# Expert preparation inside the attention's tail: where tiles lie, who prepares the first inputs, and which engine computes z from chunk 8

## The chip, the cores and the metric

The kernel runs on one core of a Trainium2 chip. A core has a matrix engine (TensorE, PE in the profile, with PEld for its weight loads), three engines for elementwise work (VectorE or DVE, ScalarE or ACT, GpSimd or POOL) and SyncE (SP), which here only issues DMAs. Each engine takes its instructions strictly in the order in which they stand in its own queue; semaphores make it wait for others. The metric is the device time of one execution in microseconds (us), lower is better.

## The reference

Two stages follow each other: a linear recurrence over 768 tokens for 4 batches of 8 heads (state 40x40), and then a mixture of 8 experts on the 3072 tokens of 320 features that come out of it, weighted by a matrix P that is normalised eight times over rows and columns.

```python
def _attn_ref(r, k, v, w, a, b):            # 4, 8, 768, 40 each
    for t in range(S):
        y[:, :, t] = np.einsum('bhd,bhde->bhe', rt, state)
        Sa = np.einsum('bhde,bhe->bhd', state, at)
        state_decay = state * wt[:, :, None, :] - np.einsum('bhd,bhe->bhde', Sa, bt)
        state = state_decay + np.einsum('bhd,bhe->bhde', vt, kt)

def _moe_ref(x, w_gate, w1, w2):            # x 3072x320, 8 experts, 1024 hidden
    logits = x @ w_gate
    P = np.exp(logits - logits.max())
    for _ in range(8):
        P /= P.sum(1, keepdims=True) + 1e-09
        P /= P.sum(0, keepdims=True) + 1e-09
        P *= N / E
    for e in range(E):
        out += P[:, e:e + 1] * (np.maximum(x @ w1[e], 0.0) @ w2[e])
```

## The kernel before

**Attention.** The 768 tokens are cut into 12 chunks c of 64; the 4 batches b run interleaved, so that there are 48 recurrence steps. `prep` builds a chunk's matrices, groups of two chunks invert their triangular systems on VectorE (`inv_diag`, `contract`, `finish`, L182 to L365), the result goes to DRAM and back, and `tmat` (L250) makes the matrix tt from it. A recurrence step (`recur`, L268) is a chain over the engines: matmul av (L282), mask f on VectorE (L283), matmuls xc (L290), copies to x and c on ScalarE (L296, L297), matmul pu (L301), mask pm on VectorE (L303), matmul c (L308), sum ws on VectorE (L310). From ws two things follow: y (L314, GpSimd), the output, which goes to the DRAM tensor xd (L317) and into the gate matmuls lp (L338); and z (L323), the state for the next chunk, which is transposed (L328) and copied into rv on ScalarE (L330, L331). Only z is on the recurrence. It is computed by GpSimd up to chunk 8 and by VectorE from chunk 9; chunk 11 has none. The steps load rv and f from DRAM through SyncE (L271, L273).

**Experts.** Weights come in 60 pieces k (`prep_w`, L498): one load of 832 KB into a raw tile ws, four sums on GpSimd (ss, 128x256 each), casts into wh by ScalarE, and remainders by GpSimd (L519 to L529; wl and a strip of wh). Tokens come in quarters s, each of three parts u (`prep_x`, L531): loads from xd into xs, four differences xt (L545 to L550), casts into xch by ScalarE (L547, L552, L555) and remainders xcl and a strip of xch (L553 to L561). For quarter 0 all of `prep_x` but the casts is on VectorE. A block is one k for one quarter: `layer1` has 28 matmuls (L573) in seven products, sums on VectorE (L591, L597) and ReLU on ScalarE (L594); `layer2` has 36 matmuls (L638). There are 128 blocks, 8192 matmuls. `sinkhorn` (L650) normalises P while the first blocks run; it needs the last gate logits lg.

**What sets the order.** Up to block 8 (N_MAN) a list scheduler with a timeline of its own orders the instructions of every engine, attention and experts together; from block 8 on, the order is the one in which the code is written. An expert tile is placed by its pool on memory that an attention tile has held, and may be written only when the readers of that tile are done. In the kernel before, the pools stand in the order stg, x0, hp, x1 (L472 to L496), and the two raw weight tiles take turns.

Of the kernel before, what the change touches and what calls it, by code (L numbers as in the profile page):

```python
# [11 lines left out]
F32 = mybir.dt.float32  # L12
F32R = mybir.dt.float32r
# [16 lines left out]
def attention(ctx, tc, d, xd, ps, pq, pt, gs, lg):  # L30
    nc = tc.nc
    pin = ctx.enter_context(tc.tile_pool(name="a_in", bufs=1))
    inv = ctx.enter_context(tc.tile_pool(name="a_inv", bufs=1))
    sets = [ctx.enter_context(tc.tile_pool(name=f"a_set{i}", bufs=1)) for i in range(NSX)]
# [233 lines left out]
    def recur(c, b):  # L268
# [54 lines left out]
        (nc.vector if c >= 9 else nc.gpsimd).tensor_tensor(out=z, in0=ws[:, :, 64:104],  # L323
# [28 lines left out]
    gq, gcount = deque(), [0]  # L352
# [103 lines left out]
def body(ctx, tc, d, out):  # L456
# [9 lines left out]
    with ExitStack() as actx:  # L466
# [3 lines left out]
        attention(actx, tc, d, xd, ps, pq, pt, gs, lg)  # L470
# [5 lines left out]
    two = ctx.enter_context(tc.tile_pool(name="two", bufs=1))  # L476
# [10 lines left out]
    xch, xcl, whs, wls = [], [], [], []
    for i in range(NWS):
        if i < SC:
            pool = x1 if i else x0  # L490
            xch.append(pool.tile([128, 7, 2, 384], F32R, name=f"xch{i}"))
            xcl.append(pool.tile([128, 7, 384], F32R, name=f"xcl{i}"))
        pool = x0 if i < 2 else x1
        whs.append(pool.tile([128, 2432], F32R, name=f"wh{i}"))
        wls.append(pool.tile([128, 1536], F32R, name=f"wl{i}"))
    acc = x1.tile([128, NT * SC, DM], F32, name="acc")  # L496

    def prep_w(k):  # L498
        e, f = (k // FP if k < E * FP else 2 * E - 2 - k // FP), k % FP
        raw = stg.tile([128, 1664], F32, name="ws")  # L500
        nc.sync.dma_start(out=raw, in_=d["wts"][e, f])
        yield
        so = stg.tile([128, 4, 2, 128], F32, name="ss", bufs=1)
# [323 lines left out]
```

## Time and profile before

| | us |
|---|---|
| median of 3 runs | 1811.9 (1807.26 to 1816.87) |
| the profiled execution | 1813.25 |
| its span in the trace | 1811.3 |
| busy in the span: PE / PEld | 1691.7 / 1668.9 |
| busy in the span: DVE / POOL / ACT | 1361.3 / 868.8 / 842.0 |
| mean granted clock of PE | 0.951 |

Times in the trace count from the start of the span. A row of the timeline has the start, the duration, the engine, the line, the operation, output and inputs, the shape and how many instructions were merged; in brackets stands how long the engine idled before it and what it waited for. A matmul group x8 of this trace is four matmuls in the code. A row of the stage table has the stage, its length, then for PE, PEld, DVE, ACT and POOL the busy time and the number of instructions, the granted clock of PE (1.00 is full speed), the share of DMA engines busy, and GB/s.

### The profile page before, as it was taken

The page shows a single profiled execution, that of the slowest core. Times are in us where ns is not written, and L with a number is a line of the kernel's source. Part 1 is how long each engine was busy: PE and PEld are TensorE (multiplying, and loading weights), DVE is VectorE, ACT ScalarE, POOL GpSimd, SP SyncE. Part 2 cuts the span into 40 slices and gives each one's busy share as a digit, 9 for nine tenths or more (in the row PEclk, how much of TensorE's full clock was granted, in tenths as well). Part 3 has the DMA queues.
Part 4 walks back from the last instruction along what each step waited for, and adds up shares of the span by engine and source line. Part 5 has one row for each costly group of instructions (what it writes and reads, how often), then busy time and mean ns, then how long its engine had stood idle before and what let it go on. Part 6 is the DMA issues. An engine that isn't in the chain of part 4 may idle for free.

```text
span 1811.3 us, 32736 instructions
## 1 busy us (share of the span) xinstructions
PE 1691.7 (93%) x12611; PEld 1668.9 (92%) x12611; DVE 1361.3 (75%) x2353; ACT 842.0 (46%) x1811; POOL 868.8 (48%) x850
## 2 busy tenths in 40 slices
PE   5468978898889999999999999999999999999999
PEld 4368878898888999999999999999999999999999
DVE  6887986974788677768686778867686777767675
ACT  6357767756534443434343444345343443434342
POOL 7555645614553453719173553009173553719160
PEclk8569989987899999999999999999999999999999
DMA  8478688577311111102010112202010111102001
GB/s 200 106 152 199 161 178 200 141 149 180 107 44 39 39 39 38 58 20 76 19 58 25 53 39 72 58 1 76 20 57 25 52 39 39 58 20 76 19 20 44
DMA packets 178737, 135.61 MB, mean 75 GB/s; under 512 B 119190, under 2 KB 160790, under 8 KB 178582
## 3 DMA queue, kind: packets, MB, share of 16 engines
q1 hardware_dynamic: 174901, 127.79, 27.1%
q10 hardware_dynamic: 3680, 5.74, 1.2%
q8 instruction: 99, 1.62, 0.4%
q14 instruction: 57, 0.46, 0.1%
HBM read 111.48 MB, written 22.02 MB: 74 GB/s over the span
## 4 chain that ended last, share of the span: by engine, by line
PE 75%; DVE 11%; DMA 5%; issue 3%; POOL 2%; SPq 2%; ACT 2%; ACTq 0%; DVEq 0%; POOLq 0%
PE op L638 36%; PE p L573 34%; DVE pr L194 1%; PE xc L290 1%; DVE q L128 1%; DMA lu<-ld 1%; PE pu L301 1%; SPq L248 1%; DMA inp<-in_inp_dram 1%; DVE un L197 1%; DMA rv<-in_rv_dram 1%; DVE sm L591 1%; DVE gt L197 1%; POOL ab L154 1%; DMA ld<-lt 1%
## 5 line engine op out<-in xcount | busy, mean ns | idle before, releaser
L573 PE MATMUL p<-xch,wh 128*128 128x384 f32 (+1 forms) x1792 | 605.9, 339 | 8.4 <-DVE sm L591 4.3
L594 ACT ACTIVATE hh<-sm 128x384 fp32r<-128x384 f32 x512 | 269.4, 527 | 729.9 <-DVE sm L591 729.9
L638 PE MATMUL op<-wh,hh 128*128 128x320 f32 x1536 | 477.2, 311 | 3.5 <-ACT hh L594 3.3
L638 PE MATMUL op<-wl,hh 128*128 128x320 f32 x1536 | 475.0, 310 | 0.0
L638 PE MATMUL op<-wh,hl 128*128 128x320 f32 x1536 | 468.9, 310 | 0.9 <-DVE hl L597 0.9
L519 POOL TENSOR_TENSOR wl<-ws,wh 128x640 fp32r<-128x640 f32 x60 | 102.8, 1714 | 608.9 <-ACT wh L517 608.7
L597 DVE SCALAR_TENSOR_TENSOR hl<-sm,hh 128x384 fp32r<-128x384 f32 x512 | 368.5, 753 | 1.9 <-ACT hh L594 1.3
L573 PEld LDWEIGHTS p<-xch,wh 128*128 128x128 f32 (+1 forms) x1792 | 337.7, 189 | 12.6 <-DVE sm L591 5.2
L573 PE MATMUL p<-xcl,wh 128*128 128x384 f32 x896 | 302.9, 338 | 0.0
L573 PE MATMUL p<-xch,wl 128*128 128x384 f32 x896 | 302.1, 337 | 0.0
L638 PEld LDWEIGHTS op<-wh,hh 128*128 128x128 f32 x1536 | 290.3, 189 | 4.4 <-ACT hh L594 4.4
L638 PEld LDWEIGHTS op<-wl,hh 128*128 128x128 f32 x1536 | 291.1, 190 | 0.0
L638 PEld LDWEIGHTS op<-wh,hl 128*128 128x128 f32 x1536 | 287.8, 188 | 1.3 <-DVE hl L597 1.2
L591 DVE TENSOR_TENSOR sm<-p,u 128x384 f32<-128x384 f32 x384 | 237.8, 629 | 8.9
L573 PEld LDWEIGHTS p<-xcl,wh 128*128 128x128 f32 x896 | 169.0, 189 | 0.0
L573 PEld LDWEIGHTS p<-xch,wl 128*128 128x128 f32 x896 | 168.9, 189 | 0.0
L591 DVE TENSOR_TENSOR sm<-p,p 128x384 f32<-128x384 f32 x128 | 71.3, 557 | 129.7 <-PE p L573 77.9
L591 DVE TENSOR_TENSOR p<-p,p 128x384 f32<-128x384 f32 x128 | 71.1, 555 | 103.5 <-PE p L573 103.1
L591 DVE TENSOR_TENSOR u<-p,p 128x384 f32<-128x384 f32 x128 | 70.8, 553 | 61.0 <-PE p L573 59.7
L527 POOL TENSOR_TENSOR wl<-ss,wh 128x512 fp32r<-128x512 f32 x60 | 90.2, 1503 | 31.5 <-ACT wh L524 27.4
L160 PE MATMUL ll<-ab,kb 104*128 104x128 f32 x336 | 62.0, 342 | 43.3 <-POOL ab L155 24.3
L160 PEld LDWEIGHTS ll<-ab,kb 104*128 104x128 f32 x336 | 53.9, 244 | 48.7 <-POOL ab L155 27.4
(164 smaller groups left out, 2642.7 us busy)
## 6 DMA issues: line engine op xcount, KB each, us to landing
ws<-in_wts_dram SPq DMA_DIRECT2D x60, 832.0 KB, 4.5
inp<-in_inp_dram SPq DMA_DIRECT2D x42, 451.5 KB, 4.7
rv<-in_rv_dram SPq DMA_DIRECT2D x48, 336.0 KB, 5.0
xd<-y SPq DMA_DIRECT2D x24, 224.0 KB, 2.9
ld<-lt ACTq DMA_DIRECT2D x40, 128.0 KB, 3.8
f<-in_vt_dram SPq DMA_DIRECT2D x48, 80.0 KB, 2.7
out_dram<-acc SPq DMA_DIRECT2D x42, 80.0 KB, 2.1
lu<-ld SPq DMA_DIRECT2D x24, 128.0 KB, 3.2
```

The costliest lines, as they stand in the source:

```text
L128: nc.vector.tensor_tensor_scan(out=qr.rearrange("r p t -> r (p t)"), data0=w65[:, 260:0:-1], data1=one65, initial=0.0, op0=ALU.mult, op1=A ...
L154: eng.tensor_tensor(out=ab[0:40, :, 0:64], in0=a_in[0:40], in1=g[0:40], op=ALU.mult)
L160: nc.tensor.matmul(ll[:, p], lhsT=kb[:, p], rhs=ab[:, p], start=True, stop=True)
L194: nc.vector.tensor_tensor(out=prv, in0=a.unsqueeze(2).broadcast_to([nu, n_c, n_r, n_k]), in1=m.unsqueeze(1).broadcast_to([nu, n_c, n_r, n_ ...
L197: nc.vector.tensor_reduce(out=dst, in_=prv, op=ALU.add, axis=AX.X)
L519: g.tensor_tensor(out=wl[:, 0:640], in0=raw[:, 256:896], in1=wh[:, 0:640], op=ALU.subtract)
L527: g.tensor_tensor(out=lv[:, 3:7], in0=so[:, :, 0], in1=hv[:, 3:7, 0], op=ALU.subtract)
L573: nc.tensor.matmul(o, lhsT=w_, rhs=x_, start=(j == 0), stop=(j == 3))
L591: eng.tensor_tensor(out=out, in0=x, in1=y, op=ALU.add)
L594: nc.scalar.activation(out=hh[:, f, h], in_=sm[f][:, h], func=AF.Relu)
L597: v.scalar_tensor_tensor(out=hl[:, f, h], in0=sm[f][:, h], scalar=0.0, in1=hh[:, f, h], op0=ALU.max, op1=ALU.subtract)
L638: nc.tensor.matmul(ops[i], lhsT=a[:, h, cs], rhs=w_[:, cw], start=(f == 0 and h == 0 and j == 0), stop=(last and h == 1 and j == 2))
```

## The change

Three edits, and what the scheduler makes of them.

1. Memory. Each expert tile gets a pool of its own (helper `pool`, with waits on the single attention tiles under it), and the pools stand in another order: xs, xt, the first token pair, the first raw weight tile, ss, the first weight pair, the work tiles of layer 1, and so on. The pool `a_inv` of attention moves to between set 6 and set 7. Pieces 0, 1 and 2 of the weights all use raw tile 0; from piece 3 on, the two take turns.
2. Who prepares. For quarter 0 GpSimd does all of `prep_x`, the casts too (nine new casts on GpSimd). The first two weight pieces and quarter 0 stand under `tc.issue_after(ends)`, where `ends` is GpSimd's last z: what they put on GpSimd's queue stands behind that instruction.
3. z is on VectorE from chunk 8 on, not from chunk 9. So GpSimd's last z is that of chunk 7, batch 3.

```diff
+    sets = []
+    for i in range(NSX):
+        if i == 7:
+            inv = ctx.enter_context(tc.tile_pool(name="a_inv", bufs=1))
+        sets.append(ctx.enter_context(tc.tile_pool(name=f"a_set{i}", bufs=1)))
...
-        (nc.vector if c >= 9 else nc.gpsimd).tensor_tensor(out=z, in0=ws[:, :, 64:104],
+        ends["z" if c < 8 else "v"] = (nc.vector if c >= 8 else nc.gpsimd).tensor_tensor(out=z, in0=ws[:, :, 64:104],
...
+    return ends["z"].ins
...
-    stg = ctx.enter_context(tc.tile_pool(name="stg", bufs=2))
-    x0 = ctx.enter_context(tc.tile_pool(name="x0", bufs=1))
-    hp = ctx.enter_context(tc.tile_pool(name="hp", bufs=2))
-    x1 = ctx.enter_context(tc.tile_pool(name="x1", bufs=1))
+    def pool(name, **kw):
+        return ctx.enter_context(tc.tile_pool(name=name, bufs=1, reuse_waits="tile", **kw))
...
+    xs_t = [pool(f"xs{i}").tile([128, 2, 2, 256], F32, name=f"xs{i}") for i in range(2)]
+    xt_t = pool("xt").tile([128, 4, 2, 128], F32, name="xt")
+    x_pair(0)
+    raws = [pool("ws0").tile([128, 1664], F32, name="ws0")]
+    ss_t = pool("ss").tile([128, 4, 2, 128], F32, name="ss")
+    w_pair(0)
...
-        raw = stg.tile([128, 1664], F32, name="ws")
+        raw = raws[k % 2 if k > 2 else 0]
...
-        v = nc.vector
+        v = nc.vector if s else nc.gpsimd
+        copy = nc.scalar.copy if s else nc.gpsimd.tensor_copy
...
-        nc.scalar.copy(out=xh[:, 0:3, :, cu], in_=bv)
+        copy(out=xh[:, 0:3, :, cu], in_=bv)
...
-    run(prep_w(0), prep_w(1), *(prep_x(0, u) for u in range(3)))
+    with tc.issue_after(ends):
+        run(prep_w(0), prep_w(1), *(prep_x(0, u) for u in range(3)))
```

Up to chunk 8 the queues of both kernels hold the same instructions in the same order. From there they differ at three places. Numbers behind an underscore are the scheduler's tile numbers; the changed file's lines are shifted (z is L326, y L317, product L597, weight load L524).

**GpSimd at chunk 8** (st_ and ge_ are the chunk's decay tiles, y_214 and y_215 the output tiles). Before:

```order
L314 TENSOR_TENSOR y_214<-ws,st_149 104x4x64
L323 TENSOR_TENSOR z<-ws,cc_155 104x160
L314 TENSOR_TENSOR y_214<-ws,st_150 104x4x64
L323 TENSOR_TENSOR z<-ws,cc_159 104x160
L314 TENSOR_TENSOR y_215<-ws,st_151 104x4x64
L323 TENSOR_TENSOR z<-ws,cc_163 104x160
L314 TENSOR_TENSOR y_215<-ws,st_152 104x4x64
L323 TENSOR_TENSOR z<-ws,cc_167 104x160
L314 TENSOR_TENSOR y_214<-ws,ge_156 104x4x64
L314 TENSOR_TENSOR y_214<-ws,ge_160 104x4x64
L314 TENSOR_TENSOR y_215<-ws,ge_164 104x4x64
L314 TENSOR_TENSOR y_215<-ws,ge_168 104x4x64
```

Now, from the same y on:

```order
L317 TENSOR_TENSOR y_214<-ws,st_149 104x4x64
L569 TENSOR_TENSOR xt<-xs_5504 128x256
L570 TENSOR_TENSOR xt<-xs_5504 128x256
L573 TENSOR_TENSOR xt<-xs_5504,xt 128x256
L574 TENSOR_TENSOR xt<-xs_5504,xt 128x256
L317 TENSOR_TENSOR y_214<-ws,st_150 104x4x64
L571 CAST xch_5516<-xs_5504 128x6x128
L576 CAST xch_5516<-xt 128x4x128
L579 CAST xch_5516<-xt 128x4x128
L571 CAST xch_5516<-xs_5508 128x6x128
L577 TENSOR_TENSOR xcl_5517<-xs_5504,xch_5516 128x3x128
L580 TENSOR_TENSOR xch_5516<-xs_5504,xch_5516 32x3x128
```

The four z are gone from the queue and the token preparation stands between the outputs y. Between this first y and the last y of attention there are now 61 instructions of the experts; before there were 26 of them, the first one behind ge_168.

**PE at chunk 10** (sx_169 is a step's matrix; p_5683 and p_5695 are the first two products of block 0). Before:

```order
L290 MATMUL xc_4977<-f,sx_169 104x104 x4
L290 MATMUL xc_4978<-f,sx_169 104x104 x4
L282 MATMUL av<-rv_208 104x128 x4
L328 MATMUL zt<-cst,z 40x104 x4
L257 MATMUL gp<-lt_200 32x32 x32
L308 MATMUL c_5010<-pm,bb_166 104x104 x4
L263 MATMUL op<-t_201,mt 32x32 x32
```

Now:

```order
L293 MATMUL xc_4977<-f,sx_169 104x104 x4
L293 MATMUL xc_4978<-f,sx_169 104x104 x4
L597 MATMUL p_5683<-xch_5516,wh_5529 128x384
L597 MATMUL p_5695<-xch_5516,wh_5529 128x384
L285 MATMUL av<-rv_208 104x128 x4
L260 MATMUL gp<-lt_200 32x32 x32
L331 MATMUL zt<-cst,z 40x104 x4
L311 MATMUL c_5010<-pm,bb_166 104x104 x4
L597 MATMUL p_5683<-xcl_5517,wh_5529 128x384
L597 MATMUL p_5695<-xcl_5517,wh_5529 128x384
L266 MATMUL op<-t_201,mt 32x32 x32
```

The first expert matmul stands ahead of 328 attention matmuls, where it stood ahead of 88. In front of the last gate matmul there are 60 expert matmuls, before 55.

**SyncE where the first weights are loaded.** Before:

```order
L317 DMA xd<-y_215 448x1x128
L501 DMA ws<-in_wts_dram 128x1664 x2
L536 DMA xs<-xd 128x2x256
L538 DMA xs<-xd 32x2x256
L273 DMA f<-in_vt_dram 64x8x40
```

Now:

```order
L560 DMA xs_5504<-xd 128x2x256
L274 DMA rv_210<-in_rv_dram 112x4x192
L562 DMA xs_5504<-xd 32x2x256
L524 DMA ws_5521<-in_wts_dram 128x1664
L276 DMA f<-in_vt_dram 64x8x40
L274 DMA rv_211<-in_rv_dram 112x4x192
```

The first weight piece moves ahead, to between the loads rv_210 and rv_211 of an earlier step; the second stays near the old place, alone, behind the load rv_209; the third stands where the last steps' outputs are written.

More of the change, by code (lines that the diff above doesn't have):

```diff
@@ L350, in gate_step @@
                 gq.popleft()
-    gq, gcount = deque(), [0]
+    gq, gcount, ends = deque(), [0], {}
     ys = {}
@@ L469, in body, with w_pair, x_pair @@
         nc.sync.dma_start(out=gs, in_=d["gate"])
-        attention(actx, tc, d, xd, ps, pq, pt, gs, lg)
-    stg = ctx.enter_context(tc.tile_pool(name="stg", bufs=2))
-    x0 = ctx.enter_context(tc.tile_pool(name="x0", bufs=1))
-    hp = ctx.enter_context(tc.tile_pool(name="hp", bufs=2))
-    x1 = ctx.enter_context(tc.tile_pool(name="x1", bufs=1))
-    two = ctx.enter_context(tc.tile_pool(name="two", bufs=1))
+        ends = attention(actx, tc, d, xd, ps, pq, pt, gs, lg)
+    def pool(name, **kw):
+        return ctx.enter_context(tc.tile_pool(name=name, bufs=1, reuse_waits="tile", **kw))
+    def w_pair(i):
+        p = pool(f"w{i}")
+        whs[i] = p.tile([128, 2432], F32R, name=f"wh{i}")
+        wls[i] = p.tile([128, 1536], F32R, name=f"wl{i}")
+    def x_pair(i):
+        p = pool(f"x{i}")
+        xch[i] = p.tile([128, 7, 2, 384], F32R, name=f"xch{i}")
+        xcl[i] = p.tile([128, 7, 384], F32R, name=f"xcl{i}")
+    xch, xcl, whs, wls = [None] * SC, [None] * SC, [None] * NWS, [None] * NWS
+    xs_t = [pool(f"xs{i}").tile([128, 2, 2, 256], F32, name=f"xs{i}") for i in range(2)]
[4 more added lines that the diff above has]
+    w_pair(0)
+    hp = pool("hp")
+    sm_t = [hp.tile([128, 768], F32, name=f"sm{i}") for i in range(2)]
+    p_t = [hp.tile([128, 384], F32, name=x) for x in ("p1", "p5", "u2", "u3")]
+    hx = [pool("h0")]
+    w_pair(1)
+    w_pair(2)
+    raws.append(pool("ws1").tile([128, 1664], F32, name="ws1"))
+    wls[3] = pool("wl3").tile([128, 1536], F32R, name="wl3")
+    hx.append(pool("h1"))
+    hs = [tuple(p.tile([128, 2, 768], F32R, name=f"{x}{i}") for x in ("hh", "hl")) for i, p in enumerate(hx)]
+    x_pair(1)
+    whs[3] = pool("wh3").tile([128, 2432], F32R, name="wh3")
+    acc = pool("acc").tile([128, NT * SC, DM], F32, name="acc")
+    two = pool("two")
     pmat = two.tile([128, 24, E], F32, name="pmat")
@@ L481, in body @@
     nc.sync.dma_start(out=ident, in_=d["cst"][:, 232:360])
-    po = ctx.enter_context(tc.tile_pool(name="po", bufs=1, space=bass.MemoryType.PSUM))
+    po = pool("po", space=bass.MemoryType.PSUM)
     ops = [po.tile([128, DM], F32, name=f"op{i}") for i in range(4)]
-    pl = [ctx.enter_context(tc.tile_pool(name=f"pl{i}", bufs=1, space=bass.MemoryType.PSUM)) for i in range(2)]
-    pe = ctx.enter_context(tc.tile_pool(name="pe", bufs=1, space=bass.MemoryType.PSUM))
+    pl = [pool(f"pl{i}", space=bass.MemoryType.PSUM) for i in range(2)]
+    pe = pool("pe", space=bass.MemoryType.PSUM)
     ops += [pe.tile([128, DM], F32, name=f"op{i}") for i in range(4, NT)]
[L487 to L496, printed above, removed]
     def prep_w(k):
         e, f = (k // FP if k < E * FP else 2 * E - 2 - k // FP), k % FP
-        raw = stg.tile([128, 1664], F32, name="ws")
+        raw = raws[k % 2 if k > 2 else 0]
         nc.sync.dma_start(out=raw, in_=d["wts"][e, f])
         yield
-        so = stg.tile([128, 4, 2, 128], F32, name="ss", bufs=1)
+        so = ss_t
         a21, a11, a12, a22 = (raw[:, o:o + 256].rearrange("r (k m) -> r k m", k=2)
@@ L577, in layer1 @@
         v = nc.vector
-        hh = hp.tile([128, 2, 768], F32R, name="hh")
-        hl = hp.tile([128, 2, 768], F32R, name="hl")
-        sm = [hp.tile([128, 768], F32, name=f"sm{i}", bufs=1) for i in range(2)]
-        p1, p5, u2, u3 = (hp.tile([128, 384], F32, name=x, bufs=1) for x in ("p1", "p5", "u2", "u3"))
+        hh, hl = hs[n % 2]
+        sm, (p1, p5, u2, u3) = sm_t, p_t
         def prod(i):
```

10 lines of the change are left out of this document (4 added, 6 removed).

## The prediction

> **What bounds the kernel now.** I read the stages first. Columns: stage, length, busy time and number of instructions of PE, PEld, DVE, ACT, POOL, PE's granted clock, DMA share, GB/s.
>
> ```profile
> 384.00:412.00 28.00, 27.39 (x326) 26.55 (x325) 27.14 (x40) 17.92 (x47) 7.61 (x10) 1.00 0.55 118
> 412.00:430.50 18.50, 15.80 (x311) 15.21 (x310) 5.18 (x11) 10.68 (x27) 1.79 (x3) 0.91 0.80 168
> 430.50:462.60 32.10, 27.55 (x222) 26.33 (x221) 22.17 (x34) 20.97 (x45) 18.36 (x19) 0.63 0.63 181
> 462.60:488.00 25.40, 24.67 (x213) 24.25 (x212) 16.20 (x30) 12.81 (x28) 12.98 (x16) 1.00 0.32 90
> 488.00:600.00 112.00, 99.71 (x572) 95.22 (x572) 95.65 (x178) 49.99 (x100) 59.30 (x53) 0.94 0.17 53
> 600.00:1808.00 1208.00, 1207.30 (x7587) 1206.05 (x7585) 889.33 (x1516) 482.81 (x951) 549.82 (x474) 1.00 0.13 42
> ```
>
> From 600 us on, PE is never without an expert matmul: 7587 of them in 1208 us at full clock, and no other engine matters. So the kernel ends as early as that stretch begins. Whatever the change gains, it gains before; and as the queues are the same up to chunk 8, it gains after about 384. Next I read PE's timeline for the steps, by the starts of the matmuls c, one group for each recurrence step.
>
> ```profile
> 430.58 0.90 PE L308 MATMUL c<-pm,bb 128*104 128x104 f32 x8
> ...
> 436.88 2.03 PE L282 MATMUL av<-rv 104*104 104x128 f32 x8 [2.18 <-ACT rv L331]
> ...
> 440.58 1.69 PE L308 MATMUL c<-pm,bb 128*104 128x104 f32 x8
> ...
> 453.72 1.72 PE L308 MATMUL c<-pm,bb 128*104 128x104 f32 x8 [1.49 <-DVE f L283]
> ...
> 462.58 0.90 PE L308 MATMUL c<-pm,bb 128*104 128x104 f32 x8
> ...
> 466.91 0.90 PE L308 MATMUL c<-pm,bb 128*104 128x104 f32 x8
> ...
> 481.26 0.90 PE L308 MATMUL c<-pm,st 128*104 128x104 f32 x8
> ...
> 487.05 0.95 PE L338 MATMUL lp<-gs,y 104*128 104x8 f32 x8
> ```
>
> The four steps from 462.58 to 481.26 take 18.68, or 4.67 each, with expert matmuls between them. The three from 430.58 to 462.58 take 32.00. At 4.67 they would take 14.0, so **18.0 us are lost** there. ScalarE's timeline, the chain of waits, SyncE's timeline and VectorE's tell to what:
>
> ```profile
> 434.88 0.83 ACT L513 CAST wh<-ws 128x768 fp32r<-128x768 f32 x1 [4.13 <-DMA ws<-in_wts_dram]
> 435.62 0.72 ACT L517 CAST wh<-ws 128x640 fp32r<-128x640 f32 x1
> 436.25 0.28 ACT L330 COPY rv<-zt 40x160 f32<-40x160 f32 x1
> ```
>
> ```profile
> 431.07 9.19 DMA f<-in_vt_dram
> ```
>
> ```profile
> 428.71 1.09 SPq L501 DMA_DIRECT2D ws<-in_wts_dram  x2
> ```
>
> ```profile
> 442.19 1.00 DVE L545 TENSOR_TENSOR xt<-xs 128x256 f32<-128x256 f32 x1 [2.54 <-DMA xs<-xd]
> ...
> 446.77 2.02 DVE L323 TENSOR_TENSOR z<-ws,cc 104x160 f32<-104x160 f32 x1
> ```
>
> Two weight pieces and the token loads are issued together. ScalarE's cast waits 4.13 for them, with the state copies rv behind it in its queue; the small load f lands after 9.19; then the token preparation stands between the steps on VectorE, and a z takes 2.02. PE runs out of work in short pieces, and the stage's clock falls to 0.63, which doubles what a matmul costs (1.69 against 0.90 for the same group).
>
> **The change, part by part.** *Gain.* The double load, the preparation on VectorE and ScalarE's token casts leave these three steps: **-18.0** if nothing replaces them (0 if all of it comes back).
>
> *VectorE at chunk 8.* Four z move to an engine that is full: 27.14 of 28.00 in 384 to 412. Behind them stand the last inversion and its `finish`, which the matrix tt and so chunk 10 wait for.
>
> ```profile
> 410.38 0.37 DVE L362 COPY tn<-un 128x256 f32<-128x256 f32 x1
> ...
> 432.24 0.33 DVE L323 TENSOR_TENSOR z<-ws,cc 104x160 f32<-104x160 f32 x1
> ```
>
> ```profile
> L323 DVE TENSOR_TENSOR z<-ws,cc 104x160 f32<-104x160 f32 x3 | 3.2, 1063 | 0.0
> ```
>
> A z on VectorE costs 0.33 with GpSimd quiet and 1.06 on average in 430 to 490, where GpSimd works. Now GpSimd works. Four z are 1.3 to 4.2, and 8.1 at 2.02 each. I take **+3.0**, as the inversion's own two-input operations will meet GpSimd too. The cover, an idle VectorE, is missing here; from 412 on it is there (5.18 of 18.50).
>
> The skill states why ("SBUF — State Buffer", SBUF: two separate sides): a VectorE operation with two SBUF inputs and a GpSimd operation lock each other out for a whole instruction. The trace agrees for z (0.33 and 2.02). By the rule every one of the four could wait out one GpSimd instruction, and the sum would be at the upper 8.1.
>
> *GpSimd's own length.* It starts when the first xs has landed. The last pieces of it are issued behind the lt loads, at 386.3; with 1 for these pieces and 3.2 for a landing that is 390.5, by estimate.
>
> ```profile
> 384.12 2.20 SPq L241 DMA_DIRECT2D lt<-ld  x2
> ```
>
> ```profile
> xs<-xd SPq DMA_DIRECT2D x12, 256.0 KB, 3.2
> ```
>
> ```profile
> L519 POOL TENSOR_TENSOR wl<-ws,wh 128x640 fp32r<-128x640 f32 x60 | 102.8, 1714 | 608.9 <-ACT wh L517 608.7
> L527 POOL TENSOR_TENSOR wl<-ss,wh 128x512 fp32r<-128x512 f32 x60 | 90.2, 1503 | 31.5 <-ACT wh L524 27.4
> L529 POOL TENSOR_TENSOR wh<-ss,wh 32x512 fp32r<-32x512 f32 x60 | 89.2, 1487 | 4.7
> L522 POOL TENSOR_TENSOR wl<-ws,wh 128x384 fp32r<-128x384 f32 x60 | 65.6, 1094 | 4.7 <-ACT wh L513 4.6
> L511 POOL TENSOR_TENSOR ss<-ws 128x256 f32<-128x256 f32 x60 | 53.8, 896 | 15.5 <-DMA ws<-in_wts_dram 11.1
> L314 POOL TENSOR_TENSOR y<-ws,ge 104x256 f32<-104x256 f32 x31 | 28.2, 909 | 44.8 <-DVE ws L310 42.5 <-DVE g L132 1.3 <-DVE lg L342 0.8
> L90 POOL MEMSET un<- 128x1056 f32 x1 | 1.0, 984 | 0.0
> ```
>
> A third of the tokens is four 128x256 (0.90), two like L522 (1.1) and two like L527 and L529 (1.5): 8.8, times three 26.4. Two weight pieces are 10.5 each, the begun third 7.5, the next tokens' beginning 2.7, fifteen y 13.6. That makes 71.2. The nine casts (5376 elements in a row) have no row on GpSimd: at the memset's 0.93 ns an element they cost 5.0, at L519's 2.68 they cost 14.4. I take 7, nearer the memset, since a cast reads one tensor and L519 two. The skill ("GPSIMD Engine Reference", Engine selection) calls one-input operations roughly line-rate there and two-input ones half VectorE's speed; by an estimate from it the casts stand at the lower bound, and the sum would be 2 us lower.
>
> ```profile
> 432.96 0.57 SPq L271 DMA_DIRECT2D rv<-in_rv_dram  x1
> ```
>
> ```profile
> DMA to landing us min/median/max: 5.1/6.7/8.3
> ```
>
> So GpSimd would be done at 390.5 + 78.2 = 468.7, but it waits once, for the second weight piece. That is issued behind the load rv_209 (432.96), so near 434, and lands 5.1 to 8.3 later (the four weight loads of 420 to 470); by the walk GpSimd wants it at about 435: +5. The last y is done at 473.7 (471.7 to 481.1); before, it was started at 483.31.
>
> ```profile
> 483.31 0.94 POOL L314 TENSOR_TENSOR y<-ws,st 104x256 f32<-104x256 f32 x1 [4.41 <-DVE ws L310]
> ```
>
> Behind a late y stand, on PE, the gate matmuls and with them the recurrence. Three of the last gate groups come up to 2 us before their y in this walk: **+2.5** (0 to 8: with the y at 481.1 some 6 of the gain would be left, 487.05 being the last gate matmul now).
>
> *The first weights on ScalarE and PE.* They are issued near 405, behind rv_210's neighbours, and ScalarE's cast stands at about 415: landing in six leaves four us, and I cost it at nothing; without that cover it is the wait of 4.13 again. PE reaches the first products at 417 to 422, and GpSimd's strips for them are ready at about 419: nothing, or 3 at the dear cast. The second piece comes alone, but its cast stands ahead of rv copies as before: **+2.0**, between 0 and 4.13.
>
> ```profile
> 460.71 0.60 PE L573 MATMUL p<-xch,wh 128*128 128x384 f32 x2
> ```
>
> *The rest.* Five more expert matmuls are done before the last gate matmul; in the stretch from 600 a matmul takes 1207.3 / 7587 = 0.16: **-0.8**. In 488 to 600 the order on all engines is nearly the same, and the second tokens still go over VectorE there: 0, within 5 either way. The pools' new order has no instruction of its own; its worth is the earlier loads, counted above.
>
> **Sum:** -18.0 + 3.0 + 2.5 + 2.0 - 0.8 = **-11.3**. The profiled execution took 1813.25, 1.35 above the median; so 1802.0 for one like it, and about **1801** beside the runs' median.
>
> **Rivals.**
>
> *More of it is kept (1793).* PE keeps full clock from 430 on, no gate matmul waits, and block 0's first products, at 460.71 before, fill the gaps: -18.0 - 0.8 = -18.8. For it: the four clean steps at 4.67 with expert matmuls between. Against: GpSimd's length, the full VectorE, and that a gap of 2.18 stands right before the clock's fall. The Trainium skill ("TensorE: Matmul & The Clock Gate", Why this matters for your kernels) puts the limit at gaps of about 3 us; by that rule the clock would hold in the new tail, where the walk has no longer gap, and this rival would come true. The trace is stricter than the rule.
>
> *Hidden anyway (1811).* Attention ends 11 earlier, but the third weight piece, the second tokens and `sinkhorn` then meet on VectorE, and the 488 to 600 stage grows by as much. For it: VectorE is busy 95.65 of 112 there, and PE idles in it:
>
> ```profile
> 496.07 0.69 PE L573 MATMUL p<-xch,wh 128*128 128x384 f32 x1 [2.96 <-DVE sm L591]
> ```
>
> Against: those stages hold the same work, only earlier.
>
> *Slower (1826): GpSimd becomes the bound.* Single instructions of it that met VectorE cost more:
>
> ```profile
> 406.46 1.60 POOL L314 TENSOR_TENSOR y<-ws,ge 104x256 f32<-104x256 f32 x1 [2.85 <-DVE ws L310]
> ...
> 467.30 1.21 POOL L511 TENSOR_TENSOR ss<-ws 128x256 f32<-128x256 f32 x1
> ```
>
> If all did (fifteen y at 1.6, 27 of 128x256 at 1.2, the casts 14.4), 71.2 would grow to about 90 and the last y would end at 390.5 + 90 + 14.4 + 5 = 500, 17 later than it starts now. Three of these are covered, since the last gate matmul comes 2.8 behind its y today: +14. It decides from the point where the last y passes 484. For it: on this queue everything stands in one line, y included. Against: in attention's tail most VectorE operations read PSUM, and a y then costs 0.9.
>
> *It doesn't do what it says.* The loads could still wait for attention's memory. The order speaks against it: xs and ws stand 30 and more rows ahead. I give it no chance of its own; it would end as the third.
>
> **How the numbers follow.** Forecast 0.48 (1795 to 1808), more kept 0.14, hidden 0.25, slower 0.13. The range 1789 to 1814 leaves out the slower case and the far end of the better one. A measurement of this kernel tells about 0.5% from no change, 9.1 us: faster is below 1802.8, slower above 1821.0. The forecast lies nearly on that line: 0.7 of it and the better case count as faster, 0.34 + 0.14 = 0.48; the rest of it and the hidden case as the same, 0.14 + 0.25 = 0.39; slower 0.13.
>
> **What would show it.** Right: steps at about 5 us between 430 and 460 with a clock near 1.00; no wait of ScalarE for ws of 4 us; the first product near 420; the last y near 474 and the last gate matmul near 476; PE full from about 589; a stage of 112 us before it as now. Wrong: gate matmuls that idle PE for several us behind y; `finish` later than 414, where it was at 410; a first cast on GpSimd that costs more than 2; or a stage before the full stretch that grew.

## The result, and the profile after

| | median | range | ratio to the kernel before |
|---|---|---|---|
| before | 1811.9 us | 1807.26 to 1816.87 | |
| with the change | 1799.48 us | 1792.51 to 1805.79 | 0.9932 (0.9908 to 0.9956) |

The change brings 12.4 us; the forecast was 1801. The profiled execution took 1799.07 (span 1797.3). In the changed kernel lines have moved: the matmuls c are L311, the gate matmuls L341, y L317, z L326, the first expert product L597. The stages of the changed kernel, at the borders of the prediction (columns as there):

```profile
384.00:412.00 28.00, 23.05 (x210) 22.10 (x209) 25.80 (x32) 15.01 (x37) 17.00 (x18) 0.94 0.63 160
412.00:430.50 18.50, 16.83 (x270) 15.82 (x269) 7.51 (x16) 13.20 (x34) 16.21 (x20) 1.00 0.88 179
430.50:462.60 32.10, 29.87 (x387) 28.70 (x385) 15.15 (x25) 22.51 (x52) 24.19 (x28) 0.95 0.58 149
462.60:488.00 25.40, 21.90 (x150) 20.86 (x148) 18.61 (x28) 13.30 (x24) 23.92 (x25) 0.93 0.39 113
```

In 430.5 to 462.6 PE does 387 matmuls where it did 222, at a clock of 0.95 in place of 0.63. In 384 to 412 it does 210 where it did 326: that stage became worse. PE's timeline shows the same in the starts of the matmuls c (one group for each recurrence step) and of the gate matmuls lp:

```profile
385.61 0.98 PE L311 MATMUL c<-pm,st 128*104 128x104 f32 x8
392.63 1.06 PE L341 MATMUL lp<-gs,y 104*128 104x8 f32 x8 [2.37 <-POOL y L317]
393.90 1.30 PE L311 MATMUL c<-pm,st 128*104 128x104 f32 x8
...
423.81 0.90 PE L311 MATMUL c<-pm,bb 128*104 128x104 f32 x8
...
431.42 0.90 PE L311 MATMUL c<-pm,bb 128*104 128x104 f32 x8
...
450.91 1.53 PE L311 MATMUL c<-pm,bb 128*104 128x104 f32 x8
...
470.29 0.90 PE L311 MATMUL c<-pm,st 128*104 128x104 f32 x8
...
476.69 0.95 PE L341 MATMUL lp<-gs,y 104*128 104x8 f32 x8
```

The same steps started at 389.32, 421.15, 430.58, 462.58 and 481.26 before, and the last gate matmul at 487.05. The first two of these rows of the kernel before are:

```profile
389.32 0.98 PE L308 MATMUL c<-pm,st 128*104 128x104 f32 x8
...
421.15 0.98 PE L308 MATMUL c<-pm,bb 128*104 128x104 f32 x8
```

Stretch by stretch, this pair of profiles gives (the 100th and the 200th expert matmul stand here and below for the first one that starts behind 100 and behind 200 of them):

| stretch (by step) | before | after | difference |
|---|---|---|---|
| start to the step at 389.32 / 385.61 | 389.32 | 385.61 | -3.7 |
| to 421.15 / 423.81 | 31.83 | 38.20 | +6.4 |
| to 430.58 / 431.42 | 9.43 | 7.61 | -1.8 |
| to 462.58 / 450.91 | 32.00 | 19.49 | -12.5 |
| to 481.26 / 470.29 | 18.68 | 19.38 | +0.7 |
| to the last gate matmul | 5.79 | 6.40 | +0.6 |
| to the 200th expert matmul, 524.16 / 510.03 | 37.11 | 33.34 | -3.8 |
| to the end of the span | 1287.1 | 1287.3 | +0.1 |

Behind the 200th expert matmul nothing changes any more. The first line I don't count to the change: up to there the queues are in the same order. In the twelve profiles of this study that share this order (all but the two whose edits reach further up, gate_one_later and chains) the step stands anywhere between 385.61 and 394.84, with the kernel before in the middle. All of these but the kernel before have the new order of the pools, so that order alone does not fix where the step stands. From there on the difference is -10.3 in this pair; the medians, over several executions, say -12.4, and the 2 us between the two are not explained.

### The profile page after: what moved, and what is told of

Same layout as the page of the kernel before. It is cut to its first block, busy times and chain, and to the rows that moved or that the text cites. A ratio compares the mean times of both kernels' runs of the same rounds, so it can differ in the third digit from the quotient of the medians.

```text
span 1797.3 us, 32534 instructions
## 1 busy us (share of the span) xinstructions
PE 1681.7 (94%) x12611; PEld 1659.7 (92%) x12611; DVE 1344.4 (75%) x2333; ACT 836.5 (47%) x1802; POOL 894.2 (50%) x879
## 4 chain that ended last, share of the span: by engine, by line
PE 75%; DVE 11%; DMA 5%; POOL 3%; issue 3%; ACT 2%; SPq 2%; ACTq 0%; DVEq 0%; POOLq 0%
PE op L659 37%; PE p L597 34%; DVE pr L197 2%; DMA inp<-in_inp_dram 1%; DVE q L131 1%; DVE gt L200 1%; DVE ge L140 1%; DMA lu<-ld 1%; DMA ld<-lt 1%; PE xc L293 1%; DVE un L200 1%; PE pu L304 1%; DMA rv<-in_rv_dram 1%; POOL ab L157 1%; DVE ws L313 1%
## 5 line engine op out<-in xcount | busy, mean ns | idle before, releaser
L597 PE MATMUL p<-xch,wh 128*128 128x384 f32 (+1 forms) x1792 | 606.0, 340 | 8.2 <-DVE u L612 3.0
L597 PEld LDWEIGHTS p<-xch,wh 128*128 128x128 f32 (+1 forms) x1792 | 338.0, 189 | 11.9 <-DVE u L612 4.9
L597 PE MATMUL p<-xcl,wh 128*128 128x384 f32 x896 | 303.0, 338 | 0.0
L597 PE MATMUL p<-xch,wl 128*128 128x384 f32 x896 | 302.4, 337 | 0.0
L612 DVE TENSOR_TENSOR sm<-p,u 128x384 f32<-128x384 f32 x384 | 232.7, 615 | 8.8
L597 PEld LDWEIGHTS p<-xcl,wh 128*128 128x128 f32 x896 | 169.1, 189 | 0.0
L597 PEld LDWEIGHTS p<-xch,wl 128*128 128x128 f32 x896 | 169.0, 189 | 0.0
```

The costliest lines, as they stand in the source:

```text
L597: nc.tensor.matmul(o, lhsT=w_, rhs=x_, start=(j == 0), stop=(j == 3))
L612: eng.tensor_tensor(out=out, in0=x, in1=y, op=ALU.add)
```

## Experiments

The first question was which part brings the gain. My theory was that of the prediction: the tail of attention gets its steps back because VectorE and ScalarE are rid of the tokens, and z on VectorE is a price. Rivals: the early loads alone; or GpSimd's own length.

**again**: the changed kernel once more.

> The changed kernel again, to see how much of what the two profiles showed repeats. In the first pair of profiles 3.7 us of the gain lay before 384 us, where the order of all engines is the same. If that part is chance, this profile has its recurrence step of 385.61 anywhere between 385 and 390 and the ratio of the times is between 0.993 and 0.996; if it belongs to the change (the new places of the pools in memory), the step stands at 385 to 386 again and the ratio is 0.993 or less. The loss of 6.4 us between that step and the sixth after it should be there again in either case.

Measured: 1797.57 us, ratio 0.9924 (0.9909 to 0.9939). The step stands at 386.00, and the six steps behind it take 38.5, so the loss of 6.4 repeats. By that expectation (385 to 386, ratio 0.993 or less) the 3.7 us ahead of the step would belong to the change. The other profiles with the new order of the pools, whose step stands at 386.8 to 394.8, speak against that; with one profile of the kernel before it isn't settled.

**pools_only**: the pools' new order without the rest.

```diff
-        v = nc.vector if s else nc.gpsimd
-        copy = nc.scalar.copy if s else nc.gpsimd.tensor_copy
+        v = nc.vector
+        copy = nc.scalar.copy
...
-        ends["z" if c < 8 else "v"] = (nc.vector if c >= 8 else nc.gpsimd).tensor_tensor(
+        ends["z" if c < 9 else "v"] = (nc.vector if c >= 9 else nc.gpsimd).tensor_tensor(
...
-    with tc.issue_after(ends):
-        run(prep_w(0), prep_w(1), *(prep_x(0, u) for u in range(3)))
+    run(prep_w(0), prep_w(1), *(prep_x(0, u) for u in range(3)))
```

> Only the new order of the pools (with the weight tiles' new buffer rule) is kept: tokens go over VectorE and ScalarE as before, nothing is tied behind the last z, z is on VectorE from chunk 9. My theory: the gain is work taken from VectorE and ScalarE in the tail, and loads that come early are worth little by themselves; the preparation still stands between the steps, so 1806 to 1812 us, ratio 0.997 to 1.000. Rival, that the early loads carry the gain: 1798 to 1802, ratio 0.993 to 0.995.

Measured: 1816.71 us, ratio 1.0035 (1.0022 to 1.0049): slower than the kernel before, which neither side had. VectorE's and ScalarE's timelines of this run show why:

```profile
398.24 0.42 DVE L569 TENSOR_TENSOR xt<-xs 128x256 f32<-128x256 f32 x1 [6.07 <-DMA xs<-xd]
```

```profile
404.21 0.50 ACT L299 COPY x<-xc 64x416 f32<-64x416 f32 x1 [7.78 <-PE xc L293]
```

The load is issued early, so the preparation stands early in VectorE's queue too, and there it waits 6.07 us for the load. The recurrence's operations stand behind it; ScalarE and PE wait with them, and one step takes 14.4 us (394.84 to 409.23). Here the early load was worth nothing to a queue that others wait for; it moved the wait to where it hurts more. So the early loads alone don't bring the gain. Whether the other two edits would bring it with the old places in memory was not run.

**x_on_vector**: the changed kernel with only `v` and `copy` put back as in this diff, so that the tokens go over VectorE and ScalarE.

> The changed kernel with the first tokens prepared on VectorE and ScalarE as before; the pools' order and z on VectorE from chunk 8 stay. My theory: this undoes most of the tail's gain (18.0 forecast, about 12 us found between the steps) and keeps the cost of z, so 1808 to 1816 us, ratio 0.998 to 1.002. Rival, that GpSimd's share is not what brings the gain: 1797 to 1803. Between 385 and 421 us the wait of PE for a late y (2.37 us) and VectorE's product of 3.46 us should both be gone, since GpSimd has nothing but y there.

Measured: 1813.41 us, ratio 1.001 (0.9999 to 1.0022). As the theory had it: without GpSimd's share there is no gain. The wait is the same (VectorE stands 6.50 us for xs before 395.31); the long product is gone (1.43 at most), and of PE's waits for y 0.22 us is left.

**z_from_9**: the changed kernel with z on GpSimd up to chunk 8. The tie moves with the last z, so the token work stands behind the four z of chunk 8.

```diff
-        ends["z" if c < 8 else "v"] = (nc.vector if c >= 8 else nc.gpsimd).tensor_tensor(
+        ends["z" if c < 9 else "v"] = (nc.vector if c >= 9 else nc.gpsimd).tensor_tensor(
```

> The changed kernel with z on GpSimd up to chunk 8, as before; the token work so starts behind the last of these z, near 402 us in place of 389. My theory: the 6.4 us lost between 385 and 421 come back for the most part, and GpSimd ends 10 us later or more, so that the last y is done near 484, no earlier than before, and the gate matmuls wait: 1800 to 1808 us, ratio 0.994 to 0.998. Rival, that GpSimd's length has room (it waited 14 us in all for data): the last y ends near 474 again and the time falls to 1793 to 1797, ratio 0.990 to 0.992.

Measured: 1811.86 us, ratio 1.000 (0.999 to 1.0011). Both sides were wrong: the loss of 6.4 us did come back (the six steps take 30.7), attention ended 10 us earlier than in the changed kernel, the last y was done at 466.6 and not near 484, and still the whole gain is gone. GpSimd's timeline, then PE's, then the stage 460 to 488:

```profile
465.95 0.68 POOL L317 TENSOR_TENSOR y<-ws,st 104x256 f32<-104x256 f32 x1
...
481.44 1.27 POOL L585 TENSOR_TENSOR xch<-xt,xch 32x512 fp32r<-32x512 f32 x1
```

```profile
466.69 1.57 PE L341 MATMUL lp<-gs,y 104*128 104x8 f32 x8 [3.53 <-POOL y L317]
...
473.48 1.01 PE L597 MATMUL p<-xch,wh 128*128 128x384 f32 x2 [3.42 <-POOL xch L576]
481.42 0.69 PE L597 MATMUL p<-xcl,wh 128*128 128x384 f32 x1 [6.93 <-POOL xcl L583]
```

```profile
460.00:488.00 28.00, 12.79 (x53) 10.60 (x53) 8.14 (x12) 6.86 (x11) 27.27 (x31) 0.63 0.31 97
```

Attention is over and PE has nothing to do: it waits for GpSimd's third token piece, done at 482.71. GpSimd is busy 27.27 of 28 us, VectorE 8.14. GpSimd had become the bound, not by a late y but by the tokens themselves. So the theory needed a second half: the start of GpSimd's work at 389 in place of 400 is what z on VectorE buys, as long as the token work is tied behind GpSimd's last z. Without that tie the scheduler begins the token work of this kernel behind the first z of chunk 8, ahead of the other three; that order was not run, so an early start with z left on GpSimd stays an untested rival. The next run takes the early start away and leaves z where the change has it.

**start_after_y8**

```diff
-        nc.gpsimd.tensor_tensor(out=y[0:R2, :, b % 2], ...)
+        yi = nc.gpsimd.tensor_tensor(out=y[0:R2, :, b % 2], ...)
+        if (c, b) == (8, 3):
+            ends["z"] = yi
...
-        ends["z" if c < 8 else "v"] = (nc.vector if c >= 8 else nc.gpsimd).tensor_tensor(
+        ends["z" if c < 0 else "v"] = (nc.vector if c >= 8 else nc.gpsimd).tensor_tensor(
```

> z stays on VectorE from chunk 8, but GpSimd's first instruction for the tokens is tied behind its last y of chunk 8 (near 402 us) in place of its last z (near 389). So GpSimd starts as late as with z on it up to chunk 8, and z is where the change puts it. My theory after the run with z from chunk 9: the 13 us by which GpSimd starts earlier are what the change lives on, since the end of the first tokens on GpSimd sets when PE is full; so this gives it all back: 1808 to 1815 us, ratio 0.998 to 1.002, with the last of the three token pieces done near 480 us, and the recurrence steps between 385 and 421 within 2 us of the kernel before. Rival, that z on VectorE frees GpSimd's queue and that is the gain: 1796 to 1802, ratio 0.992 to 0.995.

Measured: 1819.56 us, ratio 1.0037 (1.0023 to 1.0051), slower than the 1808 to 1815 expected. The third piece is done at 491.41. So with all three token pieces on GpSimd a late start loses the whole gain, with z on either engine. With nearly the same late start (402.70 and 400.07), this kernel is 0.37% or 6.7 us slower than z_from_9, more than my 3.0 for z, of which the later start can account for up to 2.6. It is no clean price of z: the orders behind the start differ too, and the third piece ends 8.7 later. Among the six steps here, 36.9 us long (31.8 before, within 2 of which I expected them), stands a product of 6.38 us on VectorE (below, in the last section).

**z9_third_on_vector**: z_from_9, with the third token piece given to the idle VectorE.

```diff
-        v = nc.vector if s else nc.gpsimd
-        copy = nc.scalar.copy if s else nc.gpsimd.tensor_copy
+        v = nc.vector if s or u == 2 else nc.gpsimd
+        copy = nc.scalar.copy if s or u == 2 else nc.gpsimd.tensor_copy
```

> z on GpSimd up to chunk 8, and of the three token pieces the third goes over VectorE, its casts over ScalarE; GpSimd does two. In the run with z from chunk 9 attention was over at 467 us, and from there to 488 VectorE was busy 8 of 28 us while PE waited 3.4 and 6.9 us for GpSimd's third piece. My theory: that piece, 11 us of GpSimd, is what PE waited for; on an idle VectorE it is done 8 to 12 us earlier: 1796 to 1804 us, ratio 0.992 to 0.996. Rival, that the piece again stands between the recurrence steps and they stretch as in the kernel before: 1808 to 1816.

Measured: 1798.24 us, ratio 0.9925 (0.9909 to 0.9941): the third piece is done at 473.18 and the gain is back, as much as in the changed kernel, by another way: with GpSimd's start as late as in z_from_9, but a third less of the tokens on it. So what counts is when the tokens are done; the early start is one way to that. It could have been more; ScalarE's timeline shows the price:

```profile
435.67 0.83 ACT L571 CAST xch<-xs 128x768 fp32r<-128x768 f32 x1 [7.24 <-DMA xs<-xd]
436.53 0.28 ACT L333 COPY rv<-zt 40x160 f32<-40x160 f32 x1
```

The same pattern as ahead of 434.88 in the kernel before: a cast that waits for a load, with the state copies rv behind it.

**third_on_vector**: the same two lines in the changed kernel, z on VectorE from chunk 8.

> The changed kernel, but the third token piece over VectorE with its casts on ScalarE. My theory: GpSimd has room in the changed kernel (the first tokens are done at 463 us, 13 before the last gate matmul), so shortening it by 11 us brings 0 to 3, and VectorE's part between the steps costs 0 to 4: 1796 to 1803 us, ratio 0.992 to 0.995. Rival, that GpSimd's length still sets the end there too: 1788 to 1794, ratio 0.987 to 0.990.

Measured: 1803.59 us, ratio 0.9954 (0.9942 to 0.9967). This lies just beyond the slow edge of what I expected. The tokens are ready at 446, but the last gate matmul comes at 483.34, 6.7 later than in the changed kernel, and the 100th expert matmul 6.2 later. It fits this that attention, and not GpSimd's length, sets the end in the changed kernel.

**gate_one_later**: the changed kernel with the gate matmuls one y later, against PE's wait of 2.37.

```diff
-    y_b = [... for i in range(2)]
+    y_b = [... for i in range(3)]
-        pm = wk.tile([128, NP, 104], F32, name="pm")
+        pm = wk.tile([128, NP, 104], F32, name="pm", bufs=1)
-GL = 3
+GL = 5
```

> The changed kernel with the gate matmuls one y later on PE: a third y buffer, the lag of the gate queue raised by one, and one buffer for pm in place of two to make room. My theory: the waits of PE for y (2.37 us at 392, 1.25 at 446) go, and as the step from 385.6 to 393.9 was stretched by that wait, 2 to 4 us come back: 1794 to 1797 us, ratio 0.990 to 0.992. Rival, that VectorE, full from 384 to 412, is what stretches these steps and the wait only stood in its shadow: no change, 1797 to 1801, ratio 0.992 to 0.994.

Measured: 1802.49 us, ratio 0.9951 (0.9939 to 0.9962), slower than either side had it. In its profile the step that stands at 385.61 in the changed kernel stands at 391.16, and the 200th expert matmul comes 3.2 us later: 5.5 us are lost ahead of that step and some 2.3 won behind it (the step with the wait takes 5.2 in place of 8.3). The edit reaches the whole of attention (one buffer for pm, other lag), so it can't say cleanly what the wait is worth.

**z9_three_buffers** and **z9_third_three_buffers**: z_from_9 and z9_third_on_vector with a third raw token buffer.

```diff
-    xs_t = [... for i in range(2)]
+    xs_t = [... for i in range(3)]
-        xr = xs_t[u % 2]
+        xr = xs_t[u % 3]
```

> z on GpSimd up to chunk 8, and a third raw token buffer, so that the third piece's load need not wait until the first piece has been read. With z from chunk 9 GpSimd waited 9.69 us for that load (to 431.27), and its third piece was done at 481 us, attention at 467. Theory: the end of the first tokens on GpSimd sets the time there; without that wait it comes 7 to 10 us earlier, and so does the end of the kernel: 1801 to 1805 us, ratio 0.994 to 0.997. Rival, that GpSimd then waits for weights in its place, or that its order changes so that the weights come later: 1808 to 1813, ratio 0.998 to 1.001.

> z on GpSimd up to chunk 8, the third token piece over VectorE and ScalarE, and the third raw token buffer. With two buffers ScalarE's cast waited 7.24 us for that load with state copies behind it, and one recurrence step took 14.1 us (429.10 to 443.24) in place of some 6. Theory: without the wait these 7 to 8 us come back, and the kernel ends earlier than the changed one: 1789 to 1793 us, ratio 0.987 to 0.990. Rival, that attention ends earlier but the first tokens are no sooner ready, or that VectorE's part stretches another step: 1796 to 1800, ratio 0.991 to 0.994.

Measured: 1804.94 us, ratio 0.9957 (0.9944 to 0.9969), within the expectation: the third piece is done at 478.92, 3.8 us earlier than in z_from_9 (7 to 10 were expected), and the 100th expert matmul comes 7.2 earlier. And 1802.94 us, ratio 0.9958 (0.9942 to 0.9973), against the expectation: the wait of 7.24 went from where it was, but as the load now comes early, the piece stands earlier in ScalarE's and VectorE's queues, and waits there. ScalarE's cast waits 5.20 us for the load, and VectorE's remainder, which reads what that cast wrote, 4.73 (its row names another DMA). The timelines of the second, ScalarE's first:

```profile
397.77 0.83 ACT L571 CAST xch<-xs 128x768 fp32r<-128x768 f32 x1 [5.20 <-DMA xs<-xd]
```

```profile
398.69 0.56 DVE L577 TENSOR_TENSOR xcl<-xs,xch 128x384 fp32r<-128x384 f32 x1 [4.73 <-DMA xd<-y]
```

One step takes 10.8 us there (393.03 to 403.85). It is the lesson of pools_only again.

**start_after_second_y8**: the changed kernel, with GpSimd's start tied behind its second y of chunk 8 (the diff of start_after_y8 with (8, 1)). In the changed kernel, leaving out the tie to the last z altogether gives the same program, so there that tie does nothing; this one does.

> The changed kernel with GpSimd's token work tied behind its second y of chunk 8 in place of its last z: one y more goes ahead, 0.7 us of work, while the tokens' load is still landing (GpSimd idles 6.80 us for it, to 388.95). What the runs so far say: PE's hundredth expert matmul comes about 15 us behind the last gate matmul, or about 22 behind the end of the third token piece on GpSimd, whichever is later (changed kernel: 476.7 and 463.3, matmul at 491.8; z from chunk 9: 466.7 and 482.7, at 504.5), and the end of the kernel 1286 us behind the two-hundredth. Theory: the wait of PE for a late y (2.37 us at 392.6) goes, the steps from 385 to 401 come 2 to 3 us earlier, attention is what sets the time in the changed kernel, so 1793 to 1797 us, ratio 0.989 to 0.991, better than both kernels. Rival, that the start matters to the microsecond or that VectorE's products meet GpSimd in another way, as in the run with the start behind the fourth y (6.38 us for one product): 1798 to 1806 us, ratio 0.992 to 0.997.

Measured: 1798.38 us, ratio 0.9928 (0.9906 to 0.995): the same as the changed kernel, as the rival had it. Attention did what the theory said and more: the six steps take 33.7 in place of 38.2, PE no longer waits for y, no product takes over 1.45, and from the step at 390.71 the last gate matmul comes after 79.4 us, in place of 91.1. But the order of GpSimd's work changed with the start; its timeline:

```profile
393.12 1.59 POOL L317 TENSOR_TENSOR y<-ws,st 104x256 f32<-104x256 f32 x1 [5.88 <-DMA xs<-xd]
...
468.01 1.26 POOL L587 TENSOR_TENSOR xch<-xt,xch 32x512 fp32r<-32x512 f32 x1
469.35 0.68 POOL L317 TENSOR_TENSOR y<-ws,st 104x256 f32<-104x256 f32 x1
```

The third piece is now done at 469.27, 5.9 later than in the changed kernel, and the 100th expert matmul at 494.99 comes 25.7 behind it. What attention gave, the tokens took.

**Two bounds.** All profiled runs but chains (below) side by side (us; the expert matmuls are counted in the trace):

| run | ratio | last gate matmul | third piece done | 100th | 200th | span |
|---|---|---|---|---|---|---|
| before | 1 | 487.05 | 467.92 | 504.5 | 524.2 | 1811.3 |
| the change | 0.9932 | 476.69 | 463.34 | 491.8 | 510.0 | 1797.3 |
| again | 0.9924 | 475.69 | 462.42 | 491.7 | 508.9 | 1794.3 |
| pools_only | 1.0035 | 502.58 | 440.25 | 517.8 | 536.0 | 1823.0 |
| x_on_vector | 1.001 | 496.00 | 432.92 | 510.6 | 528.7 | 1815.6 |
| third_on_vector | 0.9954 | 483.34 | 446.37 | 498.0 | 516.3 | 1802.0 |
| gate_one_later | 0.9951 | 480.91 | 466.57 | 495.7 | 513.3 | 1800.5 |
| z9_third_on_vector | 0.9925 | 478.01 | 473.18 | 494.5 | 514.6 | 1801.4 |
| z9_third_three_buffers | 0.9958 | 479.47 | 461.96 | 493.9 | 513.6 | 1800.1 |
| start_after_second_y8 | 0.9928 | 470.13 | 469.27 | 495.0 | 513.5 | 1799.2 |
| z9_three_buffers | 0.9957 | 464.66 | 478.92 | 497.3 | 516.7 | 1804.1 |
| z_from_9 | 1.000 | 466.69 | 482.71 | 504.5 | 520.3 | 1807.5 |
| start_after_y8 | 1.0037 | 476.99 | 491.41 | 515.5 | 532.5 | 1817.8 |

From the 200th expert matmul to the end all take 1285.3 to 1287.4. Where the tokens are ready 4.8 us or more ahead of the last gate matmul, the 100th expert matmul comes 14.5 to 17.5 behind that matmul. In the other four it comes 18 to 26 behind the third piece. So the end goes by the later of the two. This is a rule read off these thirteen profiles, and its second distance is loose: 18 to 26 is a spread as large as most of the gain. By it the change has the two some 6 us apart: 476.7 + 15 and 463.3 + 22. It fits this that no single further edit won anything: each moved one of the two, at the other's cost or out of its sight. The ratios are those of the medians and the spans those of one execution, and these differ by some microseconds (the profiled execution of pools_only took 8 more than its median).

## Why the prediction was right

The time was within 2 us of the forecast, and the tail of attention is where the gain came from. That the sum fits so well is luck: the terms are off by 1 to 3 us each, in both directions. From the step at 389.32 on:

| term | forecast | measured |
|---|---|---|
| the tail's steps and the second weight load | -18.0 + 2.0 | -13.6 (421 to 481) |
| VectorE at chunk 8 | +3.0 | +6.4 (with the next line's wait) |
| gate matmuls that wait for y | +2.5 | 2.37 inside the 6.4, 1.25 inside the -13.6 |
| the last step, to the last gate matmul | | +0.6 |
| the rest | -0.8 | -3.7 |
| sum | -11.3 | -10.3 |

- *The tail's gain* had the right place and cause (x_on_vector shows that GpSimd's share is needed), and was 2.4 too large: the three stretched steps now take 19.5, not 14.0. ScalarE's cast no longer waits 4 us for ws: it waited 0.21 at 442.60. The three steps take 5.35, 6.42 and 7.72. In the third PE waits 1.25 us for a y (446.23), and from 448.84 to 452.25 the granted clock is 0.50, although PE has no idle time over 1.25 us between 431 and 452. So the rival "more of it is kept" did not come true: the clock did not hold, though no gap came near the 3 us that it went by.
- *VectorE at chunk 8* was mis-sized. Four z took 2.5 us together, inside the 1.3 to 4.2 costed. I had the inversion meet GpSimd, but not that one product would wait out several GpSimd instructions (3.46 us; 3.45 in the run again), and not that the tokens would go ahead of y in the very first steps. The changed kernel's timelines, GpSimd's first and VectorE's behind it:

```profile
388.95 0.73 POOL L569 TENSOR_TENSOR xt<-xs 128x256 f32<-128x256 f32 x1 [6.80 <-DMA xs<-xd]
...
391.89 0.68 POOL L317 TENSOR_TENSOR y<-ws,st 104x256 f32<-104x256 f32 x1
392.52 0.82 POOL L571 CAST xch<-xs 128x768 fp32r<-128x768 f32 x1
...
395.19 1.00 POOL L577 TENSOR_TENSOR xcl<-xs,xch 128x384 fp32r<-128x384 f32 x1
396.26 1.86 POOL L580 TENSOR_TENSOR xch<-xs,xch 32x384 fp32r<-32x384 f32 x1
```

```profile
389.49 0.38 DVE L326 TENSOR_TENSOR z<-ws,cc 104x160 f32<-104x160 f32 x1
...
393.81 3.46 DVE L197 TENSOR_TENSOR pr<-un,lu 128x1024 f32<-128x1024 f32 x1
```

  A y that was due at 388 stands behind four token operations: PE waits 2.37. I expected that wait at the end, among the last gate groups; it came at the beginning. The product of 3.46 takes 1.22 elsewhere. start_after_second_y8, which has neither, recovers 4.5 of the 6.4 us.
- *GpSimd's own length* came out right, but by luck. It started at 388.95 (forecast 390.5) and the last y was done at 473.2 (473.7). In between it worked 67.8 us, where I had 78.2, and waited 14.8 in four places, where I had 5 in one (the other 1.7 are gaps of 0.08 between rows). The work was shorter because most operations took less than the means that I had read from the whole kernel (128x256: 0.73, not 0.90; a y 0.68, not 0.91). The four waits, on GpSimd's timeline:

```profile
411.81 1.49 POOL L571 CAST xch<-xs 128x768 fp32r<-128x768 f32 x1 [5.49 <-DMA ws<-in_wts_dram]
...
432.76 1.27 POOL L550 TENSOR_TENSOR wl<-ss,wh 128x512 fp32r<-128x512 f32 x1 [4.24 <-ACT wh L547]
...
442.66 0.74 POOL L534 TENSOR_TENSOR ss<-ws 128x256 f32<-128x256 f32 x1 [3.96 <-DMA ws<-in_wts_dram]
...
458.71 0.68 POOL L317 TENSOR_TENSOR y<-ws,ge 104x256 f32<-104x256 f32 x1 [1.07 <-DVE ws L313]
```

  The wait that I had forecast is the third of them. The nine casts took 6.9 us together (7 forecast), near the lower of the two bounds, on the side of "GPSIMD Engine Reference", Engine selection, of the Trainium skill, by which one-input operations run there at about line rate. The first product came at 420.18 (near 420) and the last gate matmul at 476.69 (near 476).
- *The rest* was larger by 2.9. From the last gate matmul to the 200th expert matmul PE's busy time fell from 29.7 to 29.2 us and its idle time from 7.4 to 4.2, so most of the 3.7 is idle time, which I had put at nothing (waits of 2.96 and 2.35 before, 1.66 and 2.13 now, and shorter ones). Why those waits got shorter is not known. The stage in front of the full stretch did not grow: from the 200th to the 600th expert matmul it takes 74.8 before and 74.6 after, which puts the rival "hidden anyway" out. PE is full from 589 as forecast (11.00 of 11 us in 589 to 600).

Where the reasoning was incomplete, the sum doesn't show it. I booked z on VectorE as a price only and took GpSimd's start at 390.5 as given. z_from_9 and start_after_y8 show that, with all tokens on GpSimd and the tie as it is, this start is what the price buys: without it nothing is gained. And for the slower rival I let GpSimd decide "from the point where the last y passes 484". The runs put another point ahead of it: in z_from_9 the last y is done at 466.6 and the kernel is still no faster, because PE stands 3.4 and 6.9 us for the third token piece. A walk along a queue has to end at each thing that others wait for, not only at the last one.

## What to carry to other kernels

When work is moved off the path, look for the second clock: here attention's end and the first tokens' readiness, of which the later one counts, so a change that is needed on one side shows no worth of its own unless the other side keeps up. Under a list scheduler, a transfer that is issued earlier can pull its consumer forward in an engine's queue (pools_only, x_on_vector, z9_third_three_buffers), and if that engine carries a recurrence, the wait for the transfer is then paid by the recurrence; give such work to a queue that nothing urgent shares. Where an instruction that others wait for stands in the queue right behind a newly started block of work, tie the block behind it, and then see what the block's end delays; in start_after_second_y8 that moved the loss and did not remove it.

## What was unexpected in the hardware

A VectorE operation with both inputs in SBUF (the on-chip memory that the engines work from) can wait out a whole series of GpSimd instructions. The run start_after_y8, GpSimd's timeline and then VectorE's:

```profile
402.06 0.68 POOL L317 TENSOR_TENSOR y<-ws,st 104x256 f32<-104x256 f32 x1 [4.53 <-DVE ws L313]
402.70 0.73 POOL L571 TENSOR_TENSOR xt<-xs 128x256 f32<-128x256 f32 x1
...
406.97 0.72 POOL L575 TENSOR_TENSOR xt<-xs,xt 128x256 f32<-128x256 f32 x1
```

```profile
402.40 6.38 DVE L197 TENSOR_TENSOR pr<-gt,tn 128x1024 f32<-128x1024 f32 x1
408.69 0.31 DVE L328 TENSOR_TENSOR z<-ws,cc 104x160 f32<-104x160 f32 x1
```

The product, 1.22 us elsewhere, starts while the y runs; seven more GpSimd instructions follow the y without a gap, until 407.69, and the product ends 1.09 us after the last of them. In the changed kernel the product of 3.46 ends at 397.27, 1.08 after the row that ends at 396.19. The rule that the prediction took from the Trainium skill ("SBUF — State Buffer", SBUF: two separate sides) has the loser wait out one whole instruction; these two products waited out several. But not always: in z_from_9 a product that started at 403.78, inside a cast, took 1.30 us, and in start_after_second_y8 one that started at 396.65, inside a cast too, took 1.45. The run chains was made to tell what decides.

```diff
+        n = {(8, 0): 8, (8, 1): 8, (8, 3): 12}.get((c, b), 0)
+        if n:
+            src = dum if b == 1 else cst[0:104, 0:160]
+            with tc.issue_after(zi.ins):
+                for _ in range(n):
+                    nc.gpsimd.tensor_tensor(out=dum, in0=src, in1=src, op=ALU.mult)
```

> The kernel before, with GpSimd work that nothing needs, put behind its z of chunk 8, where VectorE is full of the inversion's products (128x1024, 1.22 us each with GpSimd quiet): eight operations of 104x160 that read a constant (independent of each other) behind the first z, eight that each read what the one before wrote behind the second, twelve independent ones behind the fourth. Theory: a VectorE operation with both inputs in SBUF does not get in between GpSimd instructions that follow without a gap, but waits until such a chain ends (in the run that starts GpSimd after its y of chunk 8 a product took 6.38 us, from 402.40 to 408.78, while GpSimd ran eight instructions from 402.06 to 407.69). So the first chain (some 4 us) stretches one product to 3 to 5 us, the third to 4 to 7, and the second, where each instruction waits for the one before and leaves a gap, leaves them at 1.2 to 2. Rival, that VectorE waits for one GpSimd instruction at most, as I counted it in the prediction: no product over 1.22 + 0.45 = 1.7 us behind any of the three.

Measured, in one execution: 1827.08 us beside 1811.98, and no product waited for a chain. VectorE's timeline, then GpSimd's:

```profile
398.08 1.22 DVE L196 TENSOR_TENSOR pr<-un,lu 128x1024 f32<-128x1024 f32 x1
401.06 1.22 DVE L196 TENSOR_TENSOR pr<-un,lu 128x1024 f32<-128x1024 f32 x1
```

```profile
397.96 6.76 POOL L332 TENSOR_TENSOR dum<-cst 104x160 f32<-104x160 f32 x8
404.68 1.67 POOL L316 TENSOR_TENSOR y<-ws,st 104x256 f32<-104x256 f32 x1
```

Here GpSimd paid: eight operations of 0.45 took 6.76. The test missed its aim: all of them wrote the same tile, and they stood 0.08 us apart even where they read a constant, so there was no series without a gap. The rival (no product over 1.7) fits this run, and does not fit 6.38 and 3.46. The gap may be what let VectorE in here, but it can't be the whole of it: the products of 1.30 and 1.45 us got in between GpSimd rows that follow without one. What decides stays open.
